# A feed-forward block's second product cut by halves twice, with weight factors streamed from DRAM

## The chip, the cores and the metric

The kernel runs on one core of a Trainium2 chip. The metric is the device time of one execution in microseconds (us), the median of several runs. Names: PE is TensorE's matmuls, PEld its weight loads, DVE is VectorE, ACT is ScalarE, POOL is GpSimd, SP is SyncE, which issues the transfers (SPq is its queue).

## The reference, cut to what matters

```python
# first part: attention within hash buckets, batch 4, heads 8, sequence 768, head size 64
x = attn_out.transpose(0, 2, 1, 3).reshape(3072, 512)
# second part: 3072 tokens, d_model 512, d_ff 2048, all float32
h = x @ w_in                  # 512 -> 2048
r = np.maximum(h, 0.0)
g = r * r
out = g @ w_out               # 2048 -> 512
```

Only the second part is changed in its work.

## The kernel before

Both matrix products of the second part use a scheme of seven block products in place of eight: operands are cut into two by two blocks, sums of blocks are formed on DVE, and the helper `product` runs seven matmul groups and puts the four result blocks together. Weights and their block sums lie in SBUF for the whole kernel. Tokens come in six chunks of 512.

```python
NCH = 512                                    # tokens of a chunk; six chunks
w_in  = glob.tile([P, NFT, DFF], FP32)       # all weights stay in SBUF
w_out = glob.tile([P, NFF, DM], FP32)
...
def product(n, at, bt, c11, c12, c21, c22):
    acc = [ps_m.tile([P, 512], FP32, name=f"acc{i}")[:, 0:HN] for i in range(3)]
    def add(to, a, b, first, last):          # n matmuls into one accumulator
        ...
    def keep(of, name):                      # a copy on ScalarE
        t = p_r.tile([P, HN], FP32, name=name)
        nc.scalar.copy(out=t, in_=acc[of])
        return t
    add(0, at["11"], bt["11"], True, False)
    one = keep(0, "one")
    add(1, at["12"], bt["21"], True, True)
    c11(acc[1], one)
    add(0, at["s2"], bt["t2"], False, False) # writes acc[0]: needs the copy `one` done
    ...                                      # four more groups
...
for i in range(NCHUNK):
    for r in range(NR):                      # eight units of the first product
        if i == 0:
            sums_out(r)                      # block sums of w_out, in SBUF
        hidden(i, r)
        if i > 0 and i < 5:
            peak(i % 2, (i - 1) // 2 * NR + r)   # a maximum of |q| or |k|, for a guard
        ...
    if i + 1 < NCHUNK:
        load_x(i + 1)
        sums_x(i + 1)
    for m in range(2):
        project(i, m)                        # second product, 8 row blocks deep
```

ACT, DVE and SP work through their instructions in the order of the program. SP issues nearly all transfers.

Of the kernel before, what the change touches and what calls it, by code (L numbers as in the profile page):

```python
# [34 lines left out]
def kernel(  # L35
# [30 lines left out]
    NCH = 512  # L66
# [5 lines left out]
    w_in = glob.tile([P, NFT, DFF], FP32, name="w_in")  # L72
    w_out = glob.tile([P, NFF, DM], FP32, name="w_out")
# [6 lines left out]

    x_all = p_d.tile([P, NFT, B * S], FP32, name="x_all")

    kept_in = p_d.tile([P, NFT // 2, DFF // 2], FP32, name="kept_in")
    kept_out = p_d.tile([P, NFF // 2, DM // 2], FP32, name="kept_out")
    p_s = fast.enter_context(tc.tile_pool(name="p_s", bufs=1))
# [5 lines left out]
    p_w = first.enter_context(tc.tile_pool(name="p_w", bufs=2))  # L91
    p_v = first.enter_context(tc.tile_pool(name="p_v", bufs=2))
# [12 lines left out]
    def weight_pieces():  # L105
        for i in range(NFT):
            for c in range(0, DFF, PIECE):
                yield moe_w_in, i * P, c, w_in[:, i, c:c + PIECE]
        for i in range(NFF):
            for c in range(0, DM, PIECE):  # L110
                yield moe_w_out, i * P, c, w_out[:, i, c:c + PIECE]

    pieces = list(weight_pieces())
    raws, parts = {}, {}

    def load_weight(i):
        src, r, c, dst = pieces[i]
        if src.dtype != U64:
            nc.sync.dma_start(out=dst, in_=src[r:r + P, c:c + PIECE])
            return  # L120
        raw = p_w.tile([P, PIECE, 2], U32, name="raw", bufs=3)
        nc.sync.dma_start(
            out=raw.rearrange("p f w -> p (f w)"),
            in_=src.bitcast(U32)[r:r + P, 2 * c:2 * (c + PIECE)],
        )
        raws[i] = raw
# [28 lines left out]
    def round_weight(i):  # L155

        raw = raws.pop(i, None)
        if raw is None:
            return
# [11 lines left out]
            out=pieces[i][3], in0=one, scalar=2.0**-20, in1=power.bitcast(FP32),  # L171
            op0=ALU.mult, op1=ALU.mult,
        )

# [61 lines left out]


    nat, feat, bits = {}, {}, {}

    def load_first():  # L240

        for src, name in ((q, "q_nat"), (k, "k_nat")):
            t = p_qk.tile([P, SB, 2, D], FP32, name=name)
            for h in range(2):
                nc.sync.dma_start(
                    out=t[:, :, h], in_=src[0, h].rearrange("(p t) d -> p t d", t=SB)
                )
            nat[0, name] = t

    def load_pair(pr):  # L250
# [3 lines left out]
        for src, name in ((q, "q_nat"), (k, "k_nat")):  # L254
            t = p_qk.tile([P, S], FP32, name=name)
            for g in range(4):
                h, e = divmod(g, 2)
                nc.sync.dma_start(
                    out=t[g * 32:(g + 1) * 32].rearrange("i (t n d) -> i t n d", t=SB, n=P // 32),
                    in_=src[b, 2 * j + h].rearrange(  # L260
                        "(n i t) (e d) -> e i t n d", i=32, t=SB, e=2
                    )[e],
                )
            nat[pr, name] = t

    def load_values(pr):
# [3 lines left out]
            out=t, in_=v[b, 2 * j:2 * j + 2].rearrange("h (p t) d -> p h (t d)", t=SB)  # L270
# [188 lines left out]
    def sums_a(a11, a12, a21, a22, s1, s2, s3):  # L459
# [3 lines left out]
        nc.vector.tensor_tensor(out=a21, in0=a12, in1=s2, op=ALU.subtract)  # L463

    def sums_b(b11, b12, b21, b22, t1, t2, t3):
        nc.vector.tensor_tensor(out=t1, in0=b12, in1=b11, op=ALU.subtract)
        nc.vector.tensor_tensor(out=t3, in0=b22, in1=b12, op=ALU.subtract)
        nc.vector.tensor_tensor(out=t2, in0=b22, in1=t1, op=ALU.subtract)
        nc.vector.tensor_tensor(out=b12, in0=b21, in1=t2, op=ALU.subtract)



    HF, HD, NR = DFF // 2, DM // 2, NFF // 2
    s_in = [p_s.tile([P, NFT // 2, HF], FP32, name=f"s_in{i}") for i in range(3)]

    def sums_in(r):
        lo, hi = slice(r * P, (r + 1) * P), slice(HF + r * P, HF + (r + 1) * P)
        sums_a(
            w_in[:, 0:2, lo], w_in[:, 2:4, lo], w_in[:, 0:2, hi], w_in[:, 2:4, hi],
            *(t[:, :, lo] for t in s_in),  # L480
        )

# [15 lines left out]
    W_IN = len(pieces) // 4 * SB - 1  # L498
    for r in range(NR):
        if r == 0:  # L500
            w_steps.setdefault(W_IN + 4, []).append((sums_in, r))
        else:
            w_early.setdefault(W_IN + 1 + r * SB, []).append((sums_in, r))

    X_0 = (PB + 1) * SB
# [9 lines left out]
    def sums_x(i):  # L515
        x, t_x = xs[i]
        lo, hi = slice(0, NCH // 2), slice(NCH // 2, NCH)
        sums_b(x[:, 0:2, lo], x[:, 0:2, hi], x[:, 2:4, lo], x[:, 2:4, hi], *t_x)

    with tc.manual_schedule():  # L520
# [14 lines left out]
        for u in range(len(steps) + 1):  # L535
            for f, i in w_early.get(u, ()):
                f(i)
            if u == X_0 + SB:
                sums_x(0)
# [34 lines left out]
            if u == W_IN:  # L574
                nc.sync.dma_start(out=kept_in, in_=w_in[:, 0:2, HF:DFF])
            if u == W_IN + len(pieces) // 8 * SB:
                nc.sync.dma_start(out=kept_out, in_=w_out[:, 0:NR, HD:DM])
# [5 lines left out]
        p_o = fast.enter_context(tc.tile_pool(name="p_o", bufs=1, reuse_waits="tile"))  # L583
        t_out = [p_o.tile([P, NR, HD], FP32, name=f"t_out{i}") for i in range(3)]
        p_g = fast.enter_context(tc.tile_pool(name="p_g", bufs=1, reuse_waits="tile"))
        p_r = fast.enter_context(tc.tile_pool(name="p_r", bufs=2, reuse_waits="tile"))
        p_k = fast.enter_context(tc.tile_pool(name="p_k", bufs=2, reuse_waits="tile"))
        p_p = fast.enter_context(tc.tile_pool(name="p_p", bufs=1, reuse_waits="tile"))
        ps_m = fast.enter_context(tc.tile_pool(name="ps_m", bufs=2, space=PSUM, reuse_waits="tile"))
        ps_t = fast.enter_context(tc.tile_pool(name="ps_t", bufs=1, space=PSUM))  # L590
        HN = NCH // 2

        def sums_out(r):
            sums_b(
                w_out[:, r, 0:HD], w_out[:, r, HD:DM], w_out[:, NR + r, 0:HD],
                w_out[:, NR + r, HD:DM], *(t[:, r] for t in t_out),
            )

        def product(n, at, bt, c11, c12, c21, c22):



            acc = [ps_m.tile([P, 512], FP32, name=f"acc{i}")[:, 0:HN] for i in range(3)]

# [7 lines left out]
            def keep(of, name):  # L612
                t = p_r.tile([P, HN], FP32, name=name)
# [3 lines left out]
            add(0, at["11"], bt["11"], True, False)  # L617
            one = keep(0, "one")
            add(1, at["12"], bt["21"], True, True)
            c11(acc[1], one)  # L620
            add(0, at["s2"], bt["t2"], False, False)
            two = keep(0, "two")
            add(2, at["s1"], bt["t1"], True, False)
            five = keep(2, "five")
            add(0, at["s3"], bt["t3"], False, False)
            three = keep(0, "three")
            add(2, at["s4"], bt["22"], False, True)
            c12(acc[2], two)
            c22(three, five)
            add(0, at["22"], bt["t4"], False, True)  # L630
# [3 lines left out]
        peaks = p_p.tile([P, 2, NPK], FP32, name="peaks")  # L634
# [12 lines left out]
        top = p_p.tile([P, 2], FP32, name="top2")  # L647
# [7 lines left out]
        def guard():  # L655

            most = p_p.tile([1, 2], FP32, name="most")
# [14 lines left out]
        gates = {}  # L672

        def hidden(i, r):
# [3 lines left out]
            left, right = slice(r * P, (r + 1) * P), slice(HF + r * P, HF + (r + 1) * P)  # L678
            at = {
                "11": lambda f: w_in[:, f, left], "12": lambda f: w_in[:, 2 + f, left],  # L680
                "22": lambda f: w_in[:, 2 + f, right], "s4": lambda f: w_in[:, f, right],
            }
# [4 lines left out]
            for n in range(3):  # L687
                at[f"s{n + 1}"] = lambda f, n=n: s_in[n][:, f, left]
                bt[f"t{n + 1}"] = lambda f, n=n: t_x[n][:, f]
            g = {n: p_g.tile([P, HN], FP32, name=f"g{n}_{r}") for n in  # L690
                 ("11", "12", "21", "22", "s1", "s2", "s3")}
            gates[r] = g

            def gate(out):
                def put(one, two=None):
# [3 lines left out]
                    else:  # L699
                        nc.vector.tensor_tensor(out=h, in0=one, in1=two, op=ALU.add)  # L700
                    nc.vector.scalar_tensor_tensor(  # L701
                        out=out, in0=h, scalar=0.0, in1=h, op0=ALU.max, op1=ALU.mult
                    )
                return put



            product(2, at, bt, gate(g["11"]), gate(g["21"]), gate(g["12"]), gate(g["22"]))
            sums_a(g["11"], g["12"], g["21"], g["22"], g["s1"], g["s2"], g["s3"])
            g["s4"] = g["21"]  # L710

        def project(i, m):

            cut = slice(m * P, (m + 1) * P)
            at = {
                n: lambda r, n=n: gates[r][n][:, cut] for n in ("11", "12", "22", "s1", "s2", "s3", "s4")
            }
            bt = {
                "11": lambda r: w_out[:, r, 0:HD], "21": lambda r: w_out[:, NR + r, 0:HD],
                "22": lambda r: w_out[:, NR + r, HD:DM], "t4": lambda r: w_out[:, r, HD:DM],  # L720
            }
            for n in range(3):
                bt[f"t{n + 1}"] = lambda r, n=n: t_out[n][:, r]
            o = [p_r.tile([P, DM], FP32, name=f"o{n}", bufs=1) for n in range(2)]

            def put(out):
                def put(one, two=None):
                    if two is None:
                        nc.scalar.copy(out=out, in_=one)
                    else:  # L730
                        nc.vector.tensor_tensor(out=out, in0=one, in1=two, op=ALU.add)  # L731
                return put

            product(
                NR, at, bt, put(o[0][:, 0:HD]), put(o[0][:, HD:DM]), put(o[1][:, 0:HD]),
# [216 lines left out]
```

## Time and profile before

| | before |
|---|---|
| median | 959.32 us (959.19 to 959.94, 3 runs) |
| span of the profiled run | 956.8 us |
| first part ends | 370.7 us |
| second part, PE busy without a gap | 580.6 us |
| from PE's last matmul to the end | 5.5 us |

### The profile page before, as it was taken

What the parts mean: (1) busy time and instruction counts of PE and PEld (TensorE: products, weight loads), DVE (VectorE), ACT (ScalarE), POOL (GpSimd) and SP (SyncE); (2) the same over time, 40 slices, a digit from 0 to 9 for tenths busy, and PEclk for the clock granted to TensorE, in tenths of its full rate; (3) what the DMA queues carried; (4) which work ended last, traced back from release to release, by engine and by line L of the source; (5) the groups of instructions that cost most, each with busy time, mean ns of one, the idle gap of its engine ahead of it and who ended that gap; (6) DMA issues with size and microseconds to landing.
All of it is one profiled execution on the core that took longest, in us unless ns stands there. A gap on an engine that the chain in (4) does not pass through costs nothing.

```text
span 956.8 us, 12947 instructions
## 1 busy us (share of the span) xinstructions
PE 936.7 (98%) x5166; PEld 653.6 (68%) x5166; DVE 553.7 (58%) x1086; ACT 372.9 (39%) x685; POOL 6.0 (1%) x22
## 2 busy tenths in 40 slices
PE   5999999999999999999999999999999999999997
PEld 2333334333443436888888888888888888888886
DVE  2677778778888886970287028702870187016600
ACT  4777777777777772320131013201320132013200
POOL 2000000000000000000000000000000000000000
PEclk8999999999999999999999999999999999999999
DMA  9454464566555310010122012201220122000000
GB/s 197 89 133 111 111 170 117 123 165 134 120 146 128 101 40 17 1 44 23 57 65 77 23 56 66 77 23 55 67 77 23 56 66 77 23 23 1 1 23 25
DMA packets 121155, 70.12 MB, mean 73 GB/s; under 512 B 99328, under 2 KB 104448, under 8 KB 121088
## 3 DMA queue, kind: packets, MB, share of 16 engines
q1 hardware_dynamic: 121024, 69.22, 27.9%
q8 instruction: 42, 0.69, 0.3%
q14 instruction: 25, 0.20, 0.1%
q0 software_dynamic: 64, 0.00, 0.0%
HBM read 54.53 MB, written 14.68 MB: 72 GB/s over the span
## 4 chain that ended last, share of the span: by engine, by line
PE 96%; DVE 1%; ACT 1%; DMA 0%; issue 0%; SPq 0%; DVEq 0%; ACTq 0%
PE acc L607 61%; PE st L363 17%; PE xo L391 14%; PE tot L409 2%; PE hash L304 2%; PE tot L433 1%; ACT bits L314 0%; ACT e L368 0%; DMA q_nat<-in_q_dram 0%; PE tp L281 0%; DVE bits L325 0%; DVE feat L291 0%; DVE total L381 0%; PE st L304 0%; DVE flip L415 0%
## 5 line engine op out<-in xcount | busy, mean ns | idle before, releaser
L368 ACT ACTIVATE e<-st 128x1024 f32<-128x1024 f32 x192 | 145.5, 810 | 90.0 <-PE st L363 89.5
L607 PE MATMUL acc<-x,w_in 128*128 128x256 f32 x768 | 174.8, 379 | 0.0
L607 PE MATMUL acc<-w_out,g 128*128 128x256 f32 x768 | 168.7, 379 | 0.0
L607 PEld LDWEIGHTS acc<-w_out,g 128*128 128x128 f32 x768 | 145.9, 190 | 19.8
L607 PEld LDWEIGHTS acc<-x,w_in 128*128 128x128 f32 x768 | 145.7, 190 | 19.8
L363 PE MATMUL st<-feat,feat 64*128 64x512 f32 (+1 forms) x768 | 151.7, 487 | 0.0
L391 PE MATMUL xo<-e,v_nat 128*64 128x512 f32 (+1 forms) x768 | 144.9, 498 | 0.2 <-DVE x_t L446 0.2
L607 PE MATMUL acc<-t_x,s_in 128*128 128x256 f32 x576 | 132.2, 379 | 0.0
L607 PE MATMUL acc<-t_out,gs 128*128 128x256 f32 x576 | 126.3, 379 | 0.0
L607 PEld LDWEIGHTS acc<-t_out,gs 128*128 128x128 f32 x576 | 109.4, 190 | 14.9
L607 PEld LDWEIGHTS acc<-t_x,s_in 128*128 128x128 f32 x576 | 109.4, 190 | 14.9
L391 PEld LDWEIGHTS xo<-e,v_nat 128*64 128x64 f32 x768 | 46.9, 136 | 86.5 <-issue 84.8
L731 DVE TENSOR_TENSOR o<-acc,two 128x256 f32<-128x256 f32 x12 | 5.1, 425 | 155.4 <-PE acc L607 155.4
L363 PEld LDWEIGHTS st<-feat,feat 64*128 64x128 f32 x768 | 67.1, 191 | 34.7 <-issue 32.2
L381 DVE TENSOR_TENSOR total<-total,e 128x1536 f32<-128x1536 f32 x48 | 83.6, 1741 | 1.1 <-ACT e L368 1.0
L701 DVE SCALAR_TENSOR_TENSOR g<-h 128x256 f32<-128x256 f32 x192 | 77.3, 423 | 4.9
L614 ACT COPY two<-acc 128x256 f32<-128x256 f32 x60 | 22.4, 373 | 143.3 <-PE acc L607 143.3
L363 PE MATMUL st<-bits,bits 64*128 64x256 bf16 (+1 forms) x384 | 64.2, 330 | 7.4 <-DVE bits L329 5.4
L314 ACT ACTIVATE bits<-hash,lifts 32x384 bf16<-32x384 f32 x120 | 68.7, 573 | 4.9 <-PE hash L304 3.3
L363 PEld LDWEIGHTS <-bits 64*128 64x128 bf16 x384 | 18.9, 94 | 71.7 <-issue 65.1
L700 DVE TENSOR_TENSOR h<-acc,two 128x256 f32<-128x256 f32 x48 | 20.3, 424 | 51.5 <-PE acc L607 51.4
L614 ACT COPY one<-acc 128x256 f32<-128x256 f32 x60 | 22.4, 373 | 67.3 <-PE acc L607 67.3
(93 smaller groups left out, 613.6 us busy)
## 6 DMA issues: line engine op xcount, KB each, us to landing
raw<-in_moe_w_in_dram SPq DMA_DIRECT2D x16, 512.0 KB, 4.1
raw<-in_moe_w_out_dram SPq DMA_DIRECT2D x16, 512.0 KB, 3.5
v_nat<-in_v_dram SPq DMA_DIRECT2D x16, 384.0 KB, 3.6
x_all<-x_t SPq DMA_DIRECT2D x16, 384.0 KB, 2.6
x<-x_all SPq DMA_DIRECT2D x6, 1024.0 KB, 5.5
out_dram<-o SPq DMA_DIRECT2D x24, 256.0 KB, 2.0
raw_qk<-in_k_dram SPq DMA_DIRECT2D x16, 384.0 KB, 3.2
raw_qk<-in_q_dram SPq DMA_DIRECT2D x16, 384.0 KB, 3.2
```

The source lines that it names most:

```text
L304: nc.tensor.matmul(out=hashed[pr][h][g * NR_B:(g + 1) * NR_B, 0:HS], lhsT=projs[rows], rhs=feat[pr, w][rows, c * HS:(c + 1) * HS], start=T ...
L314: nc.scalar.activation(out=t[h * D:h * D + NR_B, c * HS:(c + 1) * HS], in_=hashed[pr][h][at, 0:HS], func=ACTF.Sign, scale=HUGE, bias=lifts ...
L363: nc.tensor.matmul(out=st[:, h, 0:hi - lo], lhsT=src[pr, 1][rows, key], rhs=src[pr, 0][rows, lo:hi], start=first, stop=not first,)
L368: nc.scalar.activation(out=e[:, :, lo:hi], in_=st[:, :, 0:hi - lo], func=ACTF.Exp, scale=scale)
L381: nc.vector.tensor_tensor(out=totals[pr], in0=in0, in1=weights[pr, kt][:, :, 0:S], op=ALU.add)
L391: nc.tensor.matmul(out=xo[h * D:(h + 1) * D, lo:hi], lhsT=nat[pr, "v_nat"][:, h, kt * D:(kt + 1) * D], rhs=weights[pr, kt][:, h, lo:hi], s ...
L409: nc.tensor.matmul(out=tot[g * 32:(g + 1) * 32, 0:HS], lhsT=ones, rhs=src[:, h, c * HS:(c + 1) * HS], start=src is totals[pr], stop=src is ...
L433: nc.tensor.matmul(out=rec, lhsT=picks, rhs=both.rearrange("p c n -> p (c n)"), start=True, stop=True)
L607: nc.tensor.matmul(out=acc[to], lhsT=a(i), rhs=b(i), start=first and i == 0, stop=last and i == n - 1, skip_group_check=True,)
L614: nc.scalar.copy(out=t, in_=acc[of])
L700: nc.vector.tensor_tensor(out=h, in0=one, in1=two, op=ALU.add)
L701: nc.vector.scalar_tensor_tensor(out=out, in0=h, scalar=0.0, in1=h, op0=ALU.max, op1=ALU.mult)
```

## The change

The intent: fewer matmul columns. The second product is cut by halves twice, so it takes 7 x 7 = 49 small products (leaves) where 7 x 8 of 64 were needed before, and chunks of 1024 tokens make the blocks wide enough. Weights and their block sums no longer lie in SBUF: the factors (blocks of a weight and sums of blocks) of both weights are prepared once, kept in DRAM and streamed in: `w_unit` (seven factors of 256 x 128, 917 KB) for each unit of the first product, `leaf` (256 KB) for each of the 49 leaves. The output comes out transposed; DVE turns 32 x 32 blocks back, and it is stored in pieces of 128 bytes. The core of the diff:

```diff
-    NCH = 512
+    NCH = 1024
...
-    w_in = glob.tile([P, NFT, DFF], FP32, name="w_in")
-    w_out = glob.tile([P, NFF, DM], FP32, name="w_out")
+    w_in_7 = p_d.tile([P, 7, NFT // 2, HF], FP32, name="w_in_7")      # in DRAM
+    w_out_49 = p_d.tile([7, P, 7, NQ, P], FP32, name="w_out_49")      # in DRAM
...
+        def load_unit(n):
+            if n < NCHUNK * NR:
+                r = n % NR
+                w_unit[n] = p_i.tile([P, 7, NFT // 2, P], FP32, name="w_unit")   # two buffers
+                nc.sync.dma_start(out=w_unit[n]..., in_=w_in_7...[:, :, r * P:(r + 1) * P])
...
+        def put_out(i, ih, jh, n, o):
+            ot = p_y.tile([P, HN], FP32, name="ot", bufs=2)
+            nc.vector.transpose(out=ot, in_=o)
+            for a in range(P // 32):
+                nc.sync.dma_start(out=out[at, ...].rearrange("(c i) j -> i c j", i=32), in_=...)
...
+        def sums_out(m):
+            t = p_1.tile([P, 2, 2, 2, 2, P], FP32, name="rows")                  # one buffer
+            nc.sync.dma_start(out=t..., in_=w_out_1[:, m:NFF:NQ])
+            f = p_1.tile([P, 7, 2, 2, P], FP32, name="factors")
+            for n, a in enumerate((a11, a12, a22)):
+                nc.scalar.copy(out=f[:, n], in_=a)
+            sums_a(...)                                                          # on DVE
+            g = p_1.tile([P, 4, 7, P], FP32, name="sums")
+            sums_a(...)
+            for n, a in enumerate((a11, a12, a22, *(g[:, n] for n in range(4)))):
+                nc.sync.dma_start(out=w_out_49[:, :, n, m]..., in_=a)
...
         for i in range(NCHUNK):
             for r in range(NR):
-                if i == 0:
-                    sums_out(r)
                 hidden(i, r)
+                load_unit(i * NR + r + 2)
+                minus(b_t[:, r], b12[:, r], b11[:, r])
+                if i == 0 and r < NQ:
+                    sums_out(r)
+                if i > 0:
+                    for n in range(2):
+                        peak(n, (i - 1) * NR + r)                                # one buffer
...
+                if r == NR - 1:
+                    for n in range(NLEAF - 2):
+                        load_leaf(n)
...
             if i + 1 < NCHUNK:
                 load_x(i + 1)
-                sums_x(i + 1)
-            for m in range(2):
-                project(i, m)
+            project(i)
+            ...                                   # then sums_x(i + 1, n), on DVE
```

## The prediction

> **What bounds the kernel now.** I read the busy shares and the chain of work that ended last first. TensorE (PE) is busy 98% of the span, and the chain runs through it nearly alone:
>
> ```profile
> PE 936.7 (98%) x5166; PEld 653.6 (68%) x5166; DVE 553.7 (58%) x1086; ACT 372.9 (39%) x685; POOL 6.0 (1%) x22
> ...
> PE 96%; DVE 1%; ACT 1%; DMA 0%; issue 0%; SPq 0%; DVEq 0%; ACTq 0%
> ```
>
> Line 607, the matmul of the `product` helper of the second part, is 61% of that chain. Next, the timeline at the border of the parts and near the end:
>
> ```profile
> 370.66 1.60 PEld L607 LDWEIGHTS acc<-x,w_in 128*128 128x128 f32 x8
> 370.68 1.97 PE L607 MATMUL acc<-x,w_in 128*128 128x256 f32 x8
> ...
> 372.95 0.33 SPq L450 DMA_DIRECT2D x_all<-x_t  x1
> ```
>
> ```profile
> 934.74 9.66 PE L607 MATMUL acc<-t_out,gs 128*128 128x256 f32 x44
> ...
> 944.24 7.07 PE L607 MATMUL acc<-w_out,g 128*128 128x256 f32 x32
> ...
> 951.39 0.37 ACT L729 COPY o<-acc 128x256 f32<-128x256 f32 x1 [6.52 <-PE acc L607]
> ```
>
> The second part runs from 370.7 to 951.3 us. Records 44 long start 9.50 us apart (944.24 - 934.74): 216 ns a record. The diff's loops give 6 x 8 x 14 = 672 matmuls in the first product and 6 x 2 x 56 = 672 in the second; each f32 matmul leaves two records (groups of 768 + 576 for either). 2688 x 216 ns = 580.6 us, exactly that stretch: PE has no gap there. Everything else waits for PE. By stretches of a chunk, 97 us each (columns: length, then busy us of PE, PEld, DVE, ACT, POOL, then clock, DMA share, GB/s):
>
> ```profile
> 376.00:473.00 97.00, 97.00 (x451) 85.40 (x450) 49.38 (x132) 18.64 (x50) 0.00 (x0) 1.00 0.09 31
> 473.00:570.00 97.00, 97.00 (x452) 85.37 (x451) 45.22 (x107) 18.64 (x50) 0.00 (x0) 1.00 0.17 55
> ```
>
> VectorE (DVE) has half its time free, ScalarE (ACT) four fifths, DMA more. So fewer matmul columns would be worth their full time, if PE can still be fed without gaps. That is the question.
>
> **What the Trainium skill says.** (1) "TensorE: Matmul & The Clock Gate", section "Wait — 56ns, not 53.3ns?": a warm matmul takes its columns over 2.4 GHz plus a fixed 2.5 ns. The trace agrees if a record of 256 f32 columns streams 512 column times: 213.3 + 2.5 = 215.8 against 216 ns. (2) The same page, section "Part 1: The HAM clock gate": after an idle window of some 3.4 us the clock is halved, until a window of sustained work. The trace agrees: PE did nearly nothing from 10 to 15.8 us, and the clock (first number after POOL) reads
>
> ```profile
> 12.00:14.00 2.00, 0.00 (x0) 0.00 (x0) 1.44 (x3) 0.44 (x1) 0.00 (x0) 0.59 0.96 138
> 14.00:16.00 2.00, 0.63 (x4) 0.54 (x6) 1.95 (x4) 0.00 (x0) 0.00 (x0) 0.50 0.98 144
> 16.00:18.00 2.00, 2.00 (x8) 0.78 (x8) 0.20 (x1) 0.26 (x1) 0.00 (x0) 0.50 1.05 151
> 18.00:20.00 2.00, 1.94 (x10) 0.80 (x10) 0.00 (x0) 1.36 (x2) 0.00 (x0) 0.70 0.90 248
> ```
>
> half until about 19.4 us, so some 3.6 us after work resumed: near 2 us lost. (3) "DMA: Bandwidth & Descriptors", sections "Anatomy of one DMA — SWDGE (gpsimd) path" and "Queues, rings and completion order": a DMA's wait for a semaphore is made by the issuing engine before dispatch, and each DMA engine takes descriptors of one queue in order. All transfers here are issued by SyncE (SP) in program order, so one waiting issue holds back all later ones. No wait in the trace of before is long enough to show it. (4) The same page, "Specifications": below 512 bytes a transfer does a read-modify-write. Reads of 128 bytes took 14.4 ns a packet in this trace's DMA records (256: 19.1; 1024: 47; 2048: 92); no write this small is in it.
>
> **The change part by part.**
>
> *First product.* 512 columns for 256: 3 x 8 x 14 x 2 = 672 records of 1024/2.4 + 2.5 = 429.2 ns: 288.4 us for 290.3. *Second product.* 3 chunks x 49 leaves x 4 matmuls x 2 = 1176 records of 216 ns: 254.0 us for 290.3. PE's work drops by 38.2 us, to 542.4. That is the whole gain, 4%.
>
> *Start of the second part.* Weights no longer lie in SBUF. The first unit (7 x 2 x 128 columns, 917 KB, 1792 pieces of 512 bytes) is issued after the last store of the first part, at 372.95 us above. How long it takes: 112 pieces a DMA engine at some 28 ns (between the 19 and 47 ns above) is 3.2 us, plus the 2.5 us by which the load of `x` exceeds its packets (32 x 92 ns = 2.9 of 5.5):
>
> ```profile
> x<-x_all SPq DMA_DIRECT2D x6, 1024.0 KB, 5.5
> out_dram<-o SPq DMA_DIRECT2D x24, 256.0 KB, 2.0
> ```
>
> 5.7 us. It lands at 379, PE was ready at 370.7: a gap of 8.4 us.
>
> *Factors of the output weights* (`sums_out`, four times in chunk 0). Program order after unit r of the first product (its last matmul ends at E): SP issues unit r+2's weights, which wait for E since there are two buffers; then the 1 MB of rows; these land at E + 5.7 + 2.8 = 8.5 us. Three ACT copies of 512 elements wait for them (0.59 us each, estimated from 373 ns at 256 and 480 at 384). ACT works in order, so the next unit's copy `one` comes after, at E + 10.9; PE needs it after two of seven products, 2 x 1.72 = 3.45 us. Gap 7.5 us. The stores of the factors (7 x 896 pieces, 392 an engine, 11 us of DMA) then delay the next unit's loads by some 3 us more. 7.5 + 3 x 10 = 37 us.
>
> *Start of each second product.* Its leaves are issued after the weights of the next unit, that is after E of the last unit. Chunk 0: 3.2 us of weight packets ahead, then a leaf's 0.7 us: first leaf at E + 6.3. Chunks 1 and 2: also after two `peak` loads with one buffer, now two for each unit; the second waits for DVE's reduction of the first. DVE per unit: seven gate operations 4.8, two reductions 1.9, differences 1.4 to 2.7, and 3.3 idle for that second load: 11.4 to 12.7 us of PE's 12.0, so it lags; the first reduction of the last unit ends near E + 9.8, the first leaf lands near E + 13. Sum 6.3 + 13 + 13 = 32 us.
>
> *Inside the second product* PE should be fed: leaves take 128 x 92 ns / 16 = 0.74 us each of DMA for 1.73 us of PE, six ahead. DVE: 53 block sums of 0.42, 28 of 1024 elements at 1.2, four of 2048 at 2.3 and eight transposes of 0.7 us, 71 us of 85: hidden. Output goes in 16384 pieces of 128 bytes a chunk within the last three of seven factors; at 15 to 20 ns 15 to 20 us beside 16 us of leaves, in 36 us: it just fits. *End of it:* next chunk's `x` sums come after the last output on DVE: 0.4 + 0.7 + 3 x 1.2 against 3.45 us of PE work: 1.5 us, twice.
>
> *Clock:* eight gaps over 6 us (1 + 4 + 3), about 2 us each: 16, less some 6 because a later start lets the stores drain. *Tail:* last matmul to end was 5.5 us; transpose, four issues of 0.5 us and small pieces add 4.
>
> **Sum.** 370.7 + 8.4 + 542.4 + 37 + 32 + 3 + 10 + 9.5 = 1013 us span; the timed run was 2.5 us above its span, so 1015. I choose 1010, a little lower, since derived gaps overlap more often than not.
>
> **Rivals.** *The gain arrives.* If SP's order hurts less (weights land sooner, or waits fall into DVE's slack) all gaps shrink to a few us: 959.3 - 38.2 + 10 to 20 = 930 to 940. For it: DVE, ACT and DMA have much room on average. Against: each gap comes from an order, not from load; even the shortest sizes (8, 4 x 5, 3 x 6) sum to 46 us, over the gain. *Gaps and gain cancel*, 945 to 978, if factors cost half. *Output writes become the bound:* if read-modify-write doubles or triples the piece's time to 40 us a chunk or more, the two `ot` buffers hold DVE, then leaves and `x` sums: 10 to 20 us a chunk, 1030 to 1060. Against: even reads this small are cheap here. *DVE becomes the bound:* its load for 1024 tokens rises from 90 us (two stretches above) to some 136 (units 8 x 6.2, peaks 15, second product 71) of PE's 181: no, save locally at the peaks.
>
> **Range and chances.** The robust part of the gaps exceeds the gain, so faster by over 2% (under 940) gets 0.06; within 2% (to 978.5) 0.18; slower 0.76. Range 972 to 1042: below if the factor gaps halve and the clock holds, above if writes are slow.
>
> **What will show it.** PE busy near 540 us in the second part, matmul groups of 128x512 (x672) and 128x256 (x1176) there; PE idle before line 607's groups of 80 us or more. The wait for `w_unit` of 8 us at 371; ACT copies `factors<-rows` waiting for DMA four times, PE then stopped 7 to 11 us each; PE or its weight load waiting for `leaf` 6 us once and 13 us twice; half clock after each. The prediction is wrong if PE shows no such gaps, if SP issues leaves before the last unit ends, or if most idle time lies inside the second product behind DVE or the output's DMA.

## More of the kernel before

The page gives shares of the span for each engine, then the granted clock of PE in 40 slices, in tenths of full speed. The slice row before:

```profile
PEclk8999999999999999999999999999999999999999
```

From 19.2 us until PE has done its last matmul the clock is full (the trace's next stretch at half clock begins at 954.4 us).

## The result, and the profile after

The changed kernel is correct and takes 1025.59 us median (1022.74 to 1028.64, 4 runs) against 959.63 us (959.19 to 959.98, 4 runs). The ratio is 1.069, 95% interval 1.066 to 1.072. Ratios here are the mean time of one kernel's runs over that of the other's of the same rounds, so not quite the ratio of the medians. It is 6.9% slower, within the range on record.

From the page of the changed kernel: busy time of the engines, the clock in slices, and the engines' shares of the chain that ended last.

```profile
PE 921.2 (90%) x4326; PEld 502.0 (49%) x4326; DVE 700.0 (68%) x1016; ACT 371.1 (36%) x607; POOL 6.0 (1%) x22
...
PEclk9999999999999978777989999999799999998998
...
PE 66%; DMA 19%; DVE 9%; issue 2%; ACT 2%; SPq 2%; DVEq 0%; ACTq 0%
```

PE has fallen from 98% to 90% of a longer span; the chain, 96% PE before, is now 19% transfers and 9% DVE; and the clock has dips that were not there. Who PE's matmuls waited for in the second part (columns: total us, times, longest; the same question gives no line at all for the kernel before):

```profile
PE acc L621 <- DMA leaf<-w_out: 34.9, 6, 11.4
PE acc L621 <- ACT one L628: 33.8, 4, 9.0
PE acc L621 <- DMA w_unit<-w_in: 8.2, 1, 8.2
PE acc L621 <- DVE t_x L484: 2.6, 2, 1.3
```

The first row is 28.5 us in three gaps where a second product starts (6.1, 11.4 and 11.1) and 6.3 us in three before its last leaf. One of the four gaps of the second row, in the timeline of all engines (columns: start, us, engine, line, operation; in brackets the idle time before it and what ended it):

```profile
394.34 0.67 SPq L891 DMA_DIRECT2D rows<-w_out  x1
...
402.80 1.66 ACT L897 COPY factors<-rows 128x512 f32<-128x512 f32 x3 [8.49 <-DMA rows<-w_out]
...
404.37 0.58 ACT L628 COPY one<-acc 128x512 f32<-128x512 f32 x1
...
405.00 7.97 PE L621 MATMUL acc<-t_x,w_unit 128*128 128x512 f32 x12 [7.87 <-ACT one L628]
```

Read it from the bottom. PE stood 7.87 us for the copy `one`. ACT could have made it by 397: PE had completed its source at about 395.4. But ACT's next instructions in order were the copies of the factors, and they waited for rows that SP had asked for only at 394.34, when the unit before had ended. The start of the second product of chunk 1, in the same view:

```profile
716.21 0.52 SPq L695 DMA_DIRECT2D w_unit<-w_in  x1
...
723.57 0.33 SPq L657 DMA_DIRECT2D raw_qk<-in_k_dram  x1
723.94 2.80 SPq L758 DMA_DIRECT2D leaf<-w_out  x6
...
727.54 4.78 PE L621 MATMUL acc<-b,leaf 128*128 128x256 f32 x13 [11.37 <-DMA leaf<-w_out]
```

Between the weights of a later unit (716.21) and the leaves that PE needs now (723.94) stands a load for the second `peak`, which has one buffer and waits for DVE. And the clock about the gap that ended at 405 (columns as in the prediction: stretch, length, busy us of PE, PEld, DVE, ACT, POOL; then clock, DMA share, GB/s):

```profile
402.00:405.00 3.00, 0.00 (x1) 0.01 (x1) 2.22 (x4) 2.14 (x4) 0.00 (x0) 0.50 0.01 3
405.00:408.00 3.00, 3.00 (x4) 1.45 (x5) 2.90 (x4) 0.00 (x0) 0.00 (x0) 0.50 0.52 154
408.00:411.00 3.00, 3.00 (x5) 1.12 (x5) 2.93 (x5) 0.59 (x1) 0.00 (x0) 0.64 0.97 283
411.00:414.00 3.00, 3.00 (x8) 1.33 (x7) 0.63 (x1) 1.17 (x2) 0.00 (x0) 1.00 0.98 282
```

PE works again from 405, but at half clock for five more us.

For the comparisons below I added up each trace the same way. Gaps: time of the second part in which no matmul runs (pieces over 0.3 us). Clock: half of PE's busy time inside the stretches that the trace records at half clock. Work: what remains of the second part. Us:

| kernel | first part ends | gaps | clock | work | tail | span |
|---|---|---|---|---|---|---|
| before | 370.7 | 0.0 | 0.0 | 580.6 | 5.5 | 956.8 |
| after | 371.8 | 79.5 | 17.9 | 545.2 | 8.5 | 1022.9 |

So PE's own work did fall by 35.4 us; 97.4 us of gaps and half clock were added.

### The profile page after: what moved, and what is told of

Same layout as the page of the kernel before. It is cut to its first block, busy times and chain, and to the rows that moved or that the text cites. A ratio compares the mean times of both kernels' runs of the same rounds, so it can differ in the third digit from the quotient of the medians.

```text
span 1022.9 us, 11731 instructions
## 1 busy us (share of the span) xinstructions
PE 921.2 (90%) x4326; PEld 502.0 (49%) x4326; DVE 700.0 (68%) x1016; ACT 371.1 (36%) x607; POOL 6.0 (1%) x22
## 4 chain that ended last, share of the span: by engine, by line
PE 66%; DMA 19%; DVE 9%; issue 2%; ACT 2%; SPq 2%; DVEq 0%; ACTq 0%
PE acc L621 33%; PE st L381 16%; PE xo L409 13%; DMA raw_qk<-in_q_dram 7%; DMA raw_qk<-in_k_dram 4%; DMA rows<-w_out 3%; PE tot L427 2%; DVE peaks L658 2%; DMA leaf<-w_out 2%; PE hash L322 2%; SPq L786 1%; DVE b L484 1%; DVE h L718 1%; DVE ot L782 1%; DVE t_x L484 1%
## 5 line engine op out<-in xcount | busy, mean ns | idle before, releaser
L621 PE MATMUL acc<-x,w_unit 128*128 128x512 f32 x384 | 170.7, 596 | 8.2 <-DMA w_unit<-w_in 8.2
L621 PE MATMUL acc<-t_x,w_unit 128*128 128x512 f32 x288 | 139.1, 636 | 36.4 <-ACT one L628 33.8
L621 PE MATMUL acc<-b,leaf 128*128 128x256 f32 x600 | 138.5, 390 | 28.5 <-DMA leaf<-w_out 28.5
L621 PEld LDWEIGHTS acc<-b,leaf 128*128 128x128 f32 x600 | 117.5, 196 | 47.8 <-DMA leaf<-w_out 31.0
L621 PEld LDWEIGHTS acc<-x,w_unit 128*128 128x128 f32 x384 | 73.4, 192 | 99.6 <-issue 98.8
L621 PEld LDWEIGHTS acc<-t_x,w_unit 128*128 128x128 f32 x288 | 58.4, 205 | 114.2 <-issue 73.8
L621 PE MATMUL acc<-t,leaf 128*128 128x256 f32 x336 | 75.9, 379 | 0.0
L621 PEld LDWEIGHTS acc<-t,leaf 128*128 128x128 f32 x336 | 63.8, 190 | 8.7
L719 DVE SCALAR_TENSOR_TENSOR b<-h 128x512 f32<-128x512 f32 x96 | 64.3, 690 | 2.5
L621 PE MATMUL acc<-b_t,leaf 128*128 128x256 f32 x240 | 54.5, 380 | 6.3 <-DMA leaf<-w_out 6.3
```

What stands on the lines that cost most here:

```text
L621: nc.tensor.matmul(out=acc[to], lhsT=a(i), rhs=b(i), start=first and i == 0, stop=last and i == n - 1, skip_group_check=True,)
L719: nc.vector.scalar_tensor_tensor(out=out[:, r], in0=h, scalar=0.0, in1=h, op0=ALU.max, op1=ALU.mult)
```

## The experiments

The theory: the loss is one of order. SP and ACT work through their instructions one by one, so a late or waiting instruction holds back others that PE needs at once; each gap then costs half clock as well. The rivals: the DMA engines or DVE are simply too heavily loaded, or the small writes of the output are slow. Ten kernels were run, each an edit of the changed kernel; all are correct but for one that is wrong.

### The copies of the factors on GpSimd (copies_pool)

```diff
-                nc.scalar.copy(out=f[:, n], in_=a)
+                nc.gpsimd.tensor_copy(out=f[:, n], in_=a)
```

> The three copies of the factors move from ScalarE to GpSimd; everything else, the late load of the rows too, stays. Theory (ScalarE works in order, so its copy one stands behind copies that wait for the rows): the four gaps of 7.9 to 9.0 us in chunk 0 (33.8 us) fall to under 1 us each, the four half-clock stretches there go with them (some 2.6 us each), so 1025.6 - 44 = 981 us (975 to 992). Rival (the weights' transfer rate or VectorE's eight sums hold TensorE): gaps of 5 us or more stay, 1010 us or more.

Measured: 1024.13 us, ratio to before 1.067 (1.065 to 1.069). A miss: nothing was gained. PE no longer waits for `one`, but it waits elsewhere. The same stretch of the timeline:

```profile
407.37 2.16 SPq L903 DMA_DIRECT2D w_out<-factors  x3
...
409.62 5.84 SPq L903 DMA_DIRECT2D w_out<-sums  x4
...
415.56 1.46 SPq L695 DMA_DIRECT2D w_unit<-w_in  x1
...
424.73 6.61 PE L621 MATMUL acc<-x,w_unit 128*128 128x512 f32 x8 [5.16 <-DMA w_unit<-w_in]
```

The unit's weights are asked for at 415.56, although their buffer was free from about 407.6, when PE's unit ended: SP was issuing stores, and the weights then stood in the queue behind them. Four such gaps, 5.2, 7.9, 9.3 and 9.5 us, take the place of the four on ACT. Behind the first wait lay a second of nearly the same length (31.9 us in all for 33.8). The claim that ACT's order alone costs 33.8 us falls.

### The rows asked for early (rows_early)

```diff
+            load_rows(m + 1)     # in sums_out, ahead of the stores; load_rows(0) before the loop
```

> The rows of the next unit are asked for as soon as their buffer is free, ahead of the stores and of the next wait of SyncE; the copies stay on ScalarE. Theory (SyncE's order makes the rows late): ScalarE's copies no longer wait, the four gaps fall to 1 us or less each, 981 us (975 to 995); the stores (11 us of DMA a unit) may make a unit's weights 1 us late. Rival (the DMA engines are too busy there, order does not matter): rows land late all the same, gaps of 5 us or more stay, 1010 us or more.

Measured: 993.93 us, ratio 1.037 (1.034 to 1.040): 31.7 us less than the changed kernel, at the edge of what was expected. The first gap is gone; three of 2.4, 2.5 and 2.2 us remain (33.8 us became 7.2), again ACT's copies, now waiting for the buffer of the factors, which is still being stored. With the loads early the stores are issued earlier too (those of the first step by 411.7 us, against 415.5 in copies_pool), so the next unit's weights are asked for sooner; that fits with this helping where moving the copies did not.

### Both together (rows_pool)

> Rows early and the copies on GpSimd together, to settle why the copies alone moved the gaps instead of removing them. Theory now (in those four units the DMA engines are the limit: per unit 3.2 us of unit weights, 2.9 of rows and 11.2 of factor stores, 17.3 us in 12 us of TensorE work, all in one queue): ScalarE no longer waits for the factors' buffer, but TensorE still stands, now for a unit's weights behind stores; gaps of 4 to 12 us in sum in units 1 to 5, and a time like rows_early's, 988 to 998 us. Rival (only ScalarE's place in the order was the cause): gaps under 2 us in sum there, 983 us or less.

Measured: 993.88 us, ratio 1.036 (1.034 to 1.038), as the theory said and not the rival. PE's waits in units 0 to 7 of chunk 0:

```profile
PE acc L621 <- DMA w_unit<-w_in: 15.7, 4, 8.5
```

8.5 of it is the gap at the border of the parts; the other three, 7.2 us, replace the 7.2 us on ACT. Whichever engine makes the copies, these units do not get their data sooner. The stretch from 400 to 458 us, first of the changed kernel, then of rows_pool (columns as in the prediction):

```profile
400.00:458.00 58.00, 35.44 (x63) 14.94 (x64) 32.80 (x44) 11.70 (x21) 0.00 (x0) 0.74 0.69 206
400.00:458.00 58.00, 50.80 (x110) 21.56 (x109) 49.66 (x65) 11.12 (x19) 9.52 (x9) 0.94 1.07 313
```

The DMA share has risen from 0.69 to 1.07 (1.06 in rows_early): by the profile's count the DMA engines have no idle time left there. What is left is consistent with the 17.3 us of DMA for each 12 us unit that the expectation adds up; it was not shown by shrinking the stores themselves.

### The leaves asked for before the last unit (leaves_early)

```diff
             for r in range(NR):
+                if r == NR - 1:
+                    for n in range(NLEAF - 2):
+                        load_leaf(n)
                 hidden(i, r)
```

> The first six leaves of each second product are asked for before the last unit of the first product instead of after it. Theory: in chunk 0 the gap of 6.1 us goes to under 1 us; in chunks 1 and 2 TensorE starts at once, does two leaves (3.45 us) and then waits for VectorE's sums, which end some 12 us after the last unit because of the two peak reductions: gaps of 11.4 and 11.1 us become 8 to 9.5 us, with VectorE named instead of the leaf's DMA. In all 6 + 2 x 2.5 + 2.6 of clock = 13 us less: 1012 us (1007 to 1018). Rival (only the load's place matters): all three gaps go, 28.5 + 8 us less, 989 us.

Measured: 1016.71 us, ratio 1.059 (1.056 to 1.062), as the theory expected. In chunk 1 the wait changes its name:

```profile
723.33 0.95 DVE L658 TENSOR_REDUCE peaks<-raw_qk 128x1 f32<-128x768 f32 x1 [3.39 <-DMA raw_qk<-in_k_dram]
724.20 0.42 DVE L484 TENSOR_TENSOR t<-b 128x256 f32<-128x256 f32 x1
724.65 0.42 DVE L484 TENSOR_TENSOR t<-b,t 128x256 f32<-128x256 f32 x1
...
725.13 2.50 PE L621 MATMUL acc<-t,leaf 128*128 128x256 f32 x5 [8.96 <-DVE t L484]
```

PE now stands 9.0 us (7.9 in chunk 2) for sums that DVE makes only after it has waited 3.4 us for the second peak's load. In chunk 0, which has no peaks, the gap at the start is gone; one of 2.5 us came up later, for a leaf queued behind the 2 MB of the next `x`.

### Leaves early and the peaks spread (leaves_peaks)

Each reduction's load is asked for right after the reduction before it, one for each unit from unit 4 of chunk 0 on, and one after each of the first six factors of the second product in chunks 0 and 1.

> As leaves_early, and the 32 peak reductions are spread: one for each unit (from unit 4 of chunk 0 on) and one after each of the first six factors of the second product in chunks 0 and 1, its load asked for one step ahead. Theory (the peaks' load, asked for only after the reduction before it, makes VectorE late): all three gaps at the start of the second product fall to under 1.5 us: 28.5 + 3 x 2.6 of clock less, 1025.6 - 36 = 989 us (983 to 996). Rival (VectorE's own work is too much there): gaps of 5 us or more stay in chunks 1 and 2, 1005 us or more.

Measured: 1004.27 us, ratio 1.049 (1.046 to 1.051): 21 us less, where 36 were expected. The long gaps at the start are gone as the theory said, so the peaks were what held DVE. But gaps fell only from 79.5 to 57.1: two of 2.5 us come from leaves behind `x`, and the gap before the last leaf grew from 2 us to 3.2 and 3.9. And the clock's loss did not fall at all (17.9 to 18.8): of its five gaps of 2.4 to 3.9 us, four are also followed by 3.4 us of half clock. My expectation had counted the clock only for long gaps.

### The first two units asked for early (unit_early)

Their two buffers get memory of their own, and the loads stand six steps before the end of the first part.

> The first two units of weights get memory of their own and are asked for six steps before the end of the first part. Theory: the gap of 8.2 us at the border goes, and the half clock after it: 1025.6 - 8.2 - 2.6 = 1015 us (1010 to 1019). Rival (the first part pays for it, its loads come later behind 1.8 MB more): the gap goes but the first part ends later, over 1020 us.

Measured: 1013.49 us, ratio 1.057 (1.055 to 1.059), as expected: the gap of 8.2 us is gone, the first part ends at 371.1 us, no later.

### Idle matmuls in the gaps (warm)

```diff
+            for n in range(9):
+                nc.tensor.matmul(out=idle[:, 0:HN], lhsT=ident, rhs=x[:, 0, lo], ...)
```

before the group that needs `one`, in units 1 to 4 of chunk 0.

> Nine idle matmuls of 512 columns (9 x 0.86 = 7.7 us, result unused) fill the four gaps of chunk 0; nothing else changes, the waits stay. Theory (each long gap costs half clock after it, the term of the sum that measured 20.9 us instead of 10): the four half-clock stretches of 10.2 us in chunk 0 disappear, and with work added the time falls by 4 x 2.6 = 10 us, to 1015 us (1010 to 1021). Rival (the clock costs nothing beyond the gap, the remainder has another cause): no change or slower by the overshoot, 1024 to 1032 us.

Measured: 1021.29 us, ratio 1.065 (1.061 to 1.068), whose interval overlaps that of the changed kernel; by time alone inconclusive. In the trace the four half-clock stretches of 10.2 us in chunk 0 became two of 3.4 us, and the clock's loss fell from 17.9 to 12.2 us, while gaps fell by 25.9 and work rose by 30.8 (the filling is longer than what it fills). The four gaps that were filled account for more than the total says: their half clock fell from 11.2 us to 3.2, some 2.0 us a gap, where 2.6 were expected; the stretches behind gaps that were not touched lost 2.2 us more than in the trace of the changed kernel. So the loss by the clock is real and comes from the gaps.

### The output in wide pieces (wide_out)

Wrong result: each block of 128 x 512 is stored as 128 pieces of 2 KB in one transfer.

> Wrong result on purpose: each output block is stored as 128 pieces of 2 KB in one transfer instead of 2048 pieces of 128 bytes in four. Theory (the small pieces are cheap and hidden but for the last leaf of each chunk and the tail): the three gaps of 2.0, 1.9 and 2.4 us before the last leaf go, and 2 to 3 us at the end: 1017 us (1012 to 1021). Rival (writes under 512 bytes are slow and hold VectorE or the next chunk's loads): 20 us or more less, under 1005 us.

Measured: 1020.24 us, ratio 1.065 (1.063 to 1.066): 5 us less, within the theory's interval. The three gaps before the last leaf are gone, nothing else is: two gaps behind `x` sums grew from 1.3 to 1.9 us, and the tail fell by 0.3 us alone. The rival of slow small writes falls. In the trace of the changed kernel its 49152 output pieces of 128 bytes, the only ones of that size after 371 us, took 13.7 ns each; the 92160 reads of that size before took 16.4.

### All mends together (mended)

Rows, leaves and first units early, leaves seven ahead in place of six, peaks spread, the next chunk's `x` sums after the fourth and fifth factor and the guard before the end.

> All mends together, correct result: rows early, leaves early and seven ahead, peaks spread, first units early, the next chunk's x sums after the fourth and fifth factor, the guard before the end. Theory (all the loss is order of issue and the half clock that follows): 1025.6 less gaps of 80 us and clock of 21 us, 925 us (920 to 936), so 3.5% faster than the kernel before; TensorE idle under 5 us in the second part. Rival (the transfers or VectorE are the limit once the order is right): idle of 15 us or more stays, 940 us or more.

Measured: correct, 941.39 us (939.84 to 945.39, 5 runs), ratio to before 0.982 (0.980 to 0.984). It beats both kernels, clear of noise, but by less than expected and, against the kernel before, by less than 2%. PE's share on its page and its waits in the second part:

```profile
PE 906.3 (96%) x4326; PEld 495.8 (53%) x4326; DVE 697.1 (74%) x1016; ACT 370.7 (39%) x607; POOL 6.0 (1%) x22
```

```profile
PE acc L636 <- ACT one L643: 8.8, 3, 3.3
PE acc L636 <- DMA leaf<-w_out: 1.5, 2, 0.8
```

Two lines of its timeline say what the first row is, and a stretch of the engines' busy times says why:

```profile
399.65 1.66 ACT L922 COPY factors<-rows 128x512 f32<-128x512 f32 x3 [3.24 <-DMA w_out<-factors]
...
401.85 7.11 PE L636 MATMUL acc<-t_x,w_unit 128*128 128x512 f32 x12 [2.63 <-ACT one L643]
```

```profile
404.00:470.60 66.60, 60.48 (x130) 25.93 (x129) 48.03 (x70) 16.62 (x30) 0.00 (x0) 0.93 0.90 263
```

The copies wait until the factors of the unit before are stored, since `factors` has one buffer, and the DMA engines are busy 90% of that stretch. The time is the rival's (940 us or more), the idle time is between theory and rival: 10.2 us of gaps, 8.8 of them these three, and 5.1 us of half clock behind them. So with the order mended the transfers of the factors are the likely next limit. That it is their rate, and not the single buffer, is not shown: a second buffer for `factors` was not tried.

### The factors' steps farther apart (mended2)

```diff
-                if i == 0 and r < NQ:
-                    sums_out(r)
+                if i == 0 and r in SUMS_AT:             # 0, 2, 3, 5
+                    sums_out(SUMS_AT.index(r))
```

> As mended, with the four steps of the factors at units 0, 2, 3 and 5 of chunk 0 instead of 0 to 3. Theory (the DMA of four steps in four units was too much; spread over six it fits): of mended's three gaps (2.6, 3.3, 2.8 us, each with 1.7 us of half clock) two go, one between units 3 and 4 stays: 941.4 - 2 x 4.5 = 932 us (928 to 937). Rival (the gaps come from the order on ScalarE alone, whatever the distance): all stay, 940 us or more.

Measured: correct, 940.27 us (939.28 to 942.63, 5 runs), ratio 0.980 (0.978 to 0.981), not distinguishable from mended and on the border of 2% faster than before. A miss: two of the three gaps on ACT went and the third shrank to 0.9 us, but PE now waits 5.6 us for unit weights (4.4 once), 2.6 for leaves and 1.9 for DVE's sums, which had to be made later. Gaps stay at 10.9 us. How the last 10 us of chunk 0 are to be had is open.

All the sums (us):

| kernel | median | gaps | clock | work | tail |
|---|---|---|---|---|---|
| after | 1025.59 | 79.5 | 17.9 | 545.2 | 8.5 |
| copies_pool | 1024.13 | 77.9 | 19.2 | 545.2 | 8.4 |
| rows_early | 993.93 | 53.9 | 12.6 | 545.1 | 8.4 |
| rows_pool | 993.88 | 53.6 | 14.7 | 545.1 | 8.4 |
| leaves_early | 1016.71 | 70.5 | 19.6 | 545.5 | 8.6 |
| leaves_peaks | 1004.27 | 57.1 | 18.8 | 545.1 | 8.4 |
| unit_early | 1013.49 | 70.7 | 16.0 | 545.3 | 8.4 |
| warm | 1021.29 | 53.6 | 12.2 | 576.0 | 8.4 |
| wide_out | 1020.24 | 74.9 | 19.5 | 544.5 | 8.2 |
| mended | 941.39 | 10.2 | 5.1 | 544.0 | 8.8 |
| mended2 | 940.27 | 10.9 | 3.4 | 544.3 | 8.8 |

## Why the prediction was right or wrong

The direction, the size and nearly all places of the loss were right: 1010 us predicted, 1025.6 measured, in the range 972 to 1042. By its steps, predicted against measured in the trace:

| step | predicted, us | measured, us |
|---|---|---|
| first part | 370.7 | 371.8 |
| PE's work | 542.4 | 545.2 |
| start of the second part | 8.4 | 8.2 |
| factors, four gaps | 37 (7.5, then 10 each) | 33.8 (7.9, 8.6, 9.0, 8.4) |
| starts of the second products | 32 (6.3, 13, 13) | 28.5 (6.1, 11.4, 11.1) |
| ends of the second products | 3 | 2.6 |
| inside the second products | 0 | 6.3 |
| clock | 10 | 17.9 |
| tail | 9.5 | 8.5 |
| span | 1013 | 1022.9 |

- **PE's work.** Right: 672 records of 512 columns and 1176 of 256. The rest is 2.8 us; in mended, with few gaps, it is 1.6. Why it is not zero was not looked into.
- **The start of the second part** was right in cause and size, and unit_early took it away for the price foreseen.
- **The factors.** The chain SP, rows, ACT, `one` was right line by line. That the order was the cause, and load was not, was only half right: copies_pool shows that undoing ACT's part alone uncovers the stores in SP's queue, which the prediction had named as a mere addition of 3 us a unit; it measured about 1. And "from an order, not from load" did not hold once the rows came early: see the DMA share of 1.07 in rows_pool.
- **The starts of the second products.** Right in cause, including the peaks on DVE, which leaves_early and leaves_peaks separate. 13 us was 1.6 to 1.9 too long.
- **Inside the second product** "it just fits" was a little too kind: the last leaf's request stands behind output stores, and PE waits about 2 us for it once a chunk. The pieces themselves took 13.7 ns, not 15 to 20.
- **The clock** is the term that was mis-sized. The prediction took 2 us for each of eight gaps and then took off 6; it measured 17.9 us, 2.2 for each. The deduction for stores that drain was about the gaps, not the clock, and should not have been taken there. Two readings behind the 2 us were a little off: PE's matmuls resumed at 15.4 us, not 15.8, and the half clock ended at 19.2, not 19.4, so 3.8 us and not 3.6 after work resumed.
- **The final choice** of 1010, "a little lower, since derived gaps overlap more often than not", was not borne out; the sum of 1015 was nearer. That the sum came so near is in part luck: four gap terms and the tail were 8 us too long, and the other terms 18 us too short.
- **Rivals.** The gain does arrive when the order is mended: mended2 is 2.0% faster than before (1.9 to 2.2). Of 38.2 us of work saved, 17.7 us reach its span. The rest is 10.9 of gaps, 3.4 of clock, 3.3 of a longer tail, 1.0 of the first part and 1.9 of work. The output writes did not become the bound, and DVE held PE for more than 3 us only where it waited for the peaks' loads (leaves_early). (The two stretches behind the prediction's "90 us" of DVE add up to 94.6; nothing hung on it.)

## What to carry to other kernels

When operands move from SBUF to a stream, ask of every request what stands before it in the issuing engine's program order, and of every copy what stands before it on its engine: here averages of 36% on ACT and 68% on DVE hid 80 us of gaps on PE. Put requests for what is needed next ahead of requests that wait for something, and do not let one single-buffered load stand in front of others. After a mend, expect a second wait behind the first, and count the half clock after a gap of TensorE as part of its price: here it followed every gap of more than 2.6 us.

## What the Trainium skill lacked or had wrong

- "TensorE: Matmul & The Clock Gate", section "Part 1: The HAM clock gate", prices gaps for one kernel alone, with bursts of some 2 us between them: half of the time at half clock, 1.67 us of it at each burst. It has no price for a gap in a long stream of matmuls. Here eight gaps of 6 to 11 us cost 17.9 us of half clock on top of themselves, 2.2 us each; of the eight half-clock stretches of the second part seven were 10.24 us long and one 6.83, each reaching into the gap's end and the matmuls behind it.
- The same page, section "Why this matters for your kernels", sets the limit for idle gaps between bursts at about 3 us. Here shorter ones were enough. In the second parts of the changed kernel and its ten edits all 67 gaps of more than 2.6 us were followed by half clock (for 3.4 us after the short ones); of the 30 gaps of 1.9 to 2.5 us six were, among them one of 2.0 us in leaves_early, where one of 2.5 us was not; of the 20 shorter ones none was.
- "DMA: Bandwidth & Descriptors", section "Specifications", says that transfers below 512 bytes do a read-modify-write. No price of it showed in the packets' times: writes of 128 bytes to DRAM took 13.7 ns a piece, reads of that size in the same trace 16.4, and widening the writes to 2 KB gained 5 us in 1025.
- The same page says that the issuing engine waits before dispatch; I found no page with a figure for what an issue costs when the queue is full. A store of 896 pieces took SP 0.56 us (median of 12) as one of the first three of a step and 1.39 us (median of 16) as one of the four behind them, so that SP was held from the next request. That the full queue is the reason is inferred.
